# Linear attention times SwiGLU on one core: u's tile, GpSimd additions, ties of the late divisions and the place of x's copies

## The chip, the cores and the metric

The kernel runs on one core of one Trainium2 chip. The metric is the device time of one execution in microseconds (us), a median over several runs. The times of before were 2395.88, 2392.64 and 2393.47 us, median 2393.47. A core has a matrix engine (TensorE, PE in the profile; its weight loads are PEld), a vector engine (VectorE, DVE), a scalar engine (ScalarE, ACT), GpSimd (POOL) and SyncE (SP). Each engine works through its own queue in order. SP and GpSimd also issue the DMAs here.

## The reference

```
xn = layernorm(x)                              # x: 2048 x 1024, float32
q, k, v = split(xn @ wqkv)                     # 32 heads of 32
pq, pk = phi(q), phi(k)                        # phi(t) = where(t > 0, t + 1, exp(t)) + 1e-6
kv = sum over tokens of pk x v;  z = sum over tokens of pk
o = (pq @ kv) / (pq . z + 1e-6)
s = o @ wo
h = silu(xn @ w1) * (xn @ w3)                  # 3584 columns
out = x + s * silu(h @ w2)
```

All large products are float32. The kernel computes each as three matmuls of a reduced float32 format: an operand is split into a high part (a copy that rounds) and a low part (the rest), and high x high, high x low and low x high are added (`mm3`, lines 97 to 99).

## The kernel before, in words

**Seven products in place of eight.** Every large matrix product is cut into 2 x 2 blocks and computed by Strassen's scheme in Winograd's form: seven block products, with sums of blocks formed ahead (S1 to S4 of the left operand, T1 to T4 of the right) and sums of products behind. A left block is 128 x 128 a piece, a right block 128 x 512 a piece.

**First half ("era 1").** Tokens go in two halves of 1024. For each half, `gemm` (line 399) computes keys, values, queries and then, in 14 pairs of columns, gate (names with g) and up (names with u). The hidden rows h = silu(gate) * up are stored to DRAM (`ho_d`) by GpSimd's DMA queue, together with their sums S1 to S4: `use_up` (line 621) multiplies, and when both parts of a half are there, `sums` (line 631) runs `four_sums` (line 601), four VectorE operations on 128 x 256 each, and stores them (line 635). `pq_d` keeps the queries' phi, `r_d` the reciprocal denominators. Side work (sums of w2's blocks, the product of kv with wo, denominators, divisions) is written as `Job`s and handed out one step at a time by `catch_up` (line 387) after each product.

**The divisions.** `divide` (line 753) loads a block of queries and the matching reciprocals (four DMAs, lines 762 and 764), multiplies them (line 770, VectorE), forms the four sums (VectorE) and has GpSimd store the result (`qs_d`, line 773). Those of the second half of the tokens (16 jobs, `late_work`, line 915) are done in the second era, with two buffers, five empty steps between a job's start and its multiplication. `catch_up(*marks)` ties the step's instructions behind the marks: on the mark's engine, each comes later in the queue than the mark. It is no wait across engines.

**Second half ("era 2", from line 851).** Five segments follow each other: B0 to B3 multiply h by w2 (over 6, 6, 8 and 8 blocks of 128 hidden rows, so 3, 3, 4 and 4 pairs of blocks k), and s multiplies the divided queries by kv x wo. Each goes over 8 groups m of 256 tokens, and in a group over the seven products in the order B11, T2, B21, T1, T3, B22, T4 (the names of the right operands). The right operands of a segment stay in SBUF, one tile a name; a segment's successor is loaded and split during the last group (m = 7), each as its predecessor's last product ends (`right`, line 872: SP loads, ScalarE makes the high part, VectorE the low part). The left operands are loaded and split four products ahead (`fetch(j + AHEAD)`, `left`, line 881), in five buffers. The sums over segments stand in `acc[m]` (four blocks c11, c12, c21, c22 of 128 x 512 a group).

`layer_tokens` (line 935) is the group of B0 to B3. After product B11 (PSUM bank ba), ScalarE copies it to u (line 948); after T2 (bb), VectorE adds bb to u (line 950), ScalarE copies u into bank bc (line 951), and VectorE adds u to c12 (line 953, not in B0). The product B21 then goes on in bank ba, so it can only start when u's copy is done. T1 goes to bd, T3 adds to bc, B22 to bd (after bd was added to c22, line 945), T4 to bc; VectorE adds each to its sum (lines 945, 959, 961).

**Memory.** Era 2's pools take the place of era 1's; a tile waits until the earlier tiles at its address are done with. Era 1 has, from the start of the pools, `pb` (8 x 4 KB a partition), `pe` (3 x 2), `pc` (6 x 2 of tag "c", which hold hs among others, and 4 x 2 of tag "sg", which hold sg), `pa` (7 x 16, the left operands), `praw` (2 x 8 "raw", the loaded weights, and 3 x 4 "job"), `st`. Era 2 has `pacc` (acc0 to acc6, 56 KB), `pu` (u, 2), `pw` (7 x 16, right operands), `pacc2` (acc7, 8), `pt` (2 x 4), `px` (5 x 4). So u lies at 56 to 58 KB, on the last "sg" buffer, and acc7 at 170 to 178 KB, on the first "raw" buffer.

**The order of the work.** Instructions are put in order by a scheduler that follows a model of their times and takes what it holds ready, by priority in the order of the program. At the change of eras, `behind(late[j], first)` (lines 1023 to 1037) puts the last steps of era 1 behind the low parts of the first four right operands of B0 on VectorE: c21 behind B11's, c12 behind T2's, the sums of one half behind B21's, those of the other half behind T1's.

**x.** `lay_x(m)` (line 920) copies 256 rows of x (1 MB) from the input to the output in DRAM, tied behind the last load; s is later added to it by accumulating DMAs. This is done for groups 0 to 6, after each group of segment B2. The last group adds x itself.

Of the kernel before, what the change touches and what calls it, by code (L numbers as in the profile page):

```python
# [9 lines left out]
F32 = mybir.dt.float32  # L10
# [12 lines left out]
def tile_linear_attention_times_swiglu(  # L23
# [576 lines left out]

    def four_sums(x1, x2, s12, s34):

        a11, a21 = (x1.rearrange("p (g t s) -> p g t s", t=2, s=P)[:, :, t] for t in range(2))
        a12, a22 = (x2.rearrange("p (g t s) -> p g t s", t=2, s=P)[:, :, t] for t in range(2))
        s1, s2 = (s12.rearrange("p (g n s) -> p g n s", n=2, s=P)[:, :, n] for n in range(2))
        s3, s4 = (s34.rearrange("p (g n s) -> p g n s", n=2, s=P)[:, :, n] for n in range(2))
        yield [nc.vector.tensor_add(out=s1, in0=a21, in1=a22),
               nc.vector.tensor_sub(out=s2, in0=s1, in1=a11)]  # L608
        yield [nc.vector.tensor_sub(out=s3, in0=a11, in1=a21),
               nc.vector.tensor_sub(out=s4, in0=a12, in1=s2)]  # L610

    def hidden(h, pair):
        sg = {}
        i = [f1 > 2 * pair for f0, f1 in FB].index(True)
        k = pair - FB[i][0] // 2

        def use_gate(n, c, src):
            sg[n, c] = signed(f"sg{h}_{pair}_{n}{c}")
            nc.scalar.activation(sg[n, c], src, AF.Silu)

        def use_up(n, c, src):
            nc.vector.tensor_mul(out=sg[n, c], in0=src, in1=sg[n, c])  # L622
            halves = sg[n, c].rearrange("p (g t s) -> p g t s", t=2, s=P)
            if n == 0:
                nc.gpsimd.dma_start(out=ho_d[i][2 * h + c][:, :, 0, k], in_=halves[:, :, 0])  # L625
            else:
                nc.gpsimd.dma_start(out=ho_d[i][2 * h + c][:, :, 1:3, k], in_=halves)  # L627
            if (n, c) in ((0, 1), (1, 0)):
                sums(c)

        def sums(c):
            o = [small(f"hs{h}_{pair}_{c}_{e}") for e in range(2)]
            for e, done in enumerate(four_sums(sg[0, c], sg[1, c], *o)):
                made[f"{h}_{pair}_", c, e] = done
                nc.gpsimd.dma_start(out=ho_d[i][2 * h + c][:, :, 3 + 2 * e:5 + 2 * e, k],  # L635
                                in_=o[e].rearrange("p (g n s) -> p g n s", n=2, s=P))

        return use_gate, use_up
# [218 lines left out]
    def late_pool(name, bufs=1):  # L857
        return ctx.enter_context(tc.tile_pool(name=name, bufs=bufs, reuse_waits="tile"))

    pacc, pu, pw, pacc2, pt, px = (late_pool(*how) for how in (  # L860
        ("pacc",), ("pu",), ("pw",), ("pacc2",), ("pt", 2), ("px", 5)))

    class Segment:
# [17 lines left out]
        def left(self, m, n):  # L881
            t = px.tile([P, 2, ND // 2, P], FR, tag="x", name=f"X{PARTNER[n]}{self.name}_{m}")
            x_ = t[:, :, :self.nk]
            loads[:] = [nc.sync.dma_start(out=x_[:, 1].bitcast(F32), in_=self.left_of(m, PARTNER[n]))]
            made[m, n, self.name] = split(x_[:, e] for e in range(2))
            return x_
# [6 lines left out]
    def split(pair):  # L893
        hi, lo = pair
        src = lo.bitcast(F32)
        nc.scalar.copy(out=hi, in_=src)  # L896
        return nc.vector.tensor_sub(out=lo, in0=src, in1=hi.bitcast(F32))  # L897

# [10 lines left out]
    segments = layers + [attention]  # L909
    acc = [(pacc if m < NG - 1 else pacc2).tile([P, 2, 2, C], F32, tag=f"acc{m}", name=f"acc{m}") for m in range(NG)]  # L910

# [5 lines left out]

    jobs.append((late_work(), False))

    def lay_x(m):  # L920
# [14 lines left out]
    def layer_tokens(seg, m, first):  # L935
        name = f"{seg.name}_{m}"
        V, A = nc.vector, nc.scalar
        c11, c12, c21, c22 = (acc[m][:, t, n] for t in range(2) for n in range(2))
        ba, bb, bc, bd = (bank(f"{n}{name}") for n in "abcd")
# [12 lines left out]
        if not first:  # L952
            V.tensor_add(out=c12, in0=c12, in1=u)
        yield ba, False
# [11 lines left out]
    def attention_tokens(seg, m):  # L966
        name = f"{seg.name}_{m}"
        V, A = nc.vector, nc.scalar
        a11, a12, a21, a22 = (acc[m][:, t, n] for t in range(2) for n in range(2))
        ba, bb, bc, bd = (bank(f"{n}{name}") for n in "abcd")  # L970
# [52 lines left out]
    def behind(late, first):  # L1023
        for i in late:
            tc.add_manual_dep(i.ins, first.ins.name, mybir.DependencyInfo(
                mybir.DependencyClass.NoSync, mybir.DependencyReason.DATA))

    tail = f"{NH - 1}_{NF // 2 - 1}_"
    late = [[made["u" + tail, "c21"]], [made["u" + tail, "c12"]], made[tail, 1, 0] + made[tail, 1, 1],
            made[tail, 0, 0] + made[tail, 0, 1]]  # L1030
    with tc.high_priority(offset=150):
        for j, n in enumerate(ORDER):
            if j < AHEAD:
                fetch(j)
# [43 lines left out]
```

## Time and profile before

| what | value |
|---|---|
| median of 3 runs | 2393.47 us (2392.64 to 2395.88) |
| the profiled execution | 2394.54 us, its span 2392.8 us |
| mean granted clock of TensorE | 0.996 |
| ScalarE busy | 957.0 us, 40% |
| GpSimd busy | 287.9 us, 12% |
| VectorE busy | 1659.7 us, 69% |
| bytes moved by DMAs | 395.45 MB, mean 165 GB/s |

How to read it. Times in the trace are microseconds from the start of the span. A row of the timeline has the start, the duration, the engine, the line of the kernel, the operation, out<-in, the shapes, how many were merged, and in brackets how long the engine had been idle before and what ended that. A row of the stretches ("windows") has the stretch, its length, the busy time and number of instructions of PE, PEld, DVE, ACT and POOL, the granted clock of TensorE (1.00 is full), the DMA engines' share and GB/s. A row of the waits has the engine, what it wanted to do, whom it waited for, the total, the count and the longest. Consecutive operations of one engine overlap a little, so their distance is less than their duration. Names: XS4B is the left operand S4 in a segment B, B21B the right operand B21, aB to dB the four PSUM banks, qd the queries being divided, hs the sums and sg the product silu(gate) * up.

The product of a segment with 3 pairs of blocks is 9 matmuls, with 4 pairs 12.

### The profile page before, as it was taken

What the parts mean: (1) busy time and instruction counts of PE and PEld (TensorE: products, weight loads), DVE (VectorE), ACT (ScalarE), POOL (GpSimd) and SP (SyncE); (2) the same over time, 40 slices, a digit from 0 to 9 for tenths busy, and PEclk for the clock granted to TensorE, in tenths of its full rate; (3) what the DMA queues carried; (4) which work ended last, traced back from release to release, by engine and by line L of the source; (5) the groups of instructions that cost most, each with busy time, mean ns of one, the idle gap of its engine ahead of it and who ended that gap; (6) DMA issues with size and microseconds to landing.
All of it is one profiled execution on the core that took longest, in us unless ns stands there. A gap on an engine that the chain in (4) does not pass through costs nothing.

```text
span 2392.8 us, 29793 instructions
## 1 busy us (share of the span) xinstructions
PE 2337.6 (98%) x10544; PEld 1927.8 (81%) x10544; DVE 1659.7 (69%) x2948; ACT 957.0 (40%) x1619; POOL 287.9 (12%) x357
## 2 busy tenths in 40 slices
PE   6999999999999999999999999999999999999999
PEld 5788888888888888887888888887777778788787
DVE  8755787888887666567777787787446675754744
ACT  5434554433332244355343333344343342444532
POOL 3000111211112100000232221211000000000010
PEclk9999999999999999999999999999999999999999
DMA  3211455567664593124354556435355666833766
GB/s 124 88 53 36 158 188 165 192 224 244 228 224 145 183 336 104 64 106 132 139 176 161 188 173 200 159 113 178 99 157 176 208 238 215 282 114 97 234 150 159
DMA packets 266406, 395.45 MB, mean 165 GB/s; under 512 B 17120, under 2 KB 191456, under 8 KB 266144
## 3 DMA queue, kind: packets, MB, share of 16 engines
q1 hardware_dynamic: 238576, 302.04, 39.2%
q0 software_dynamic: 27680, 91.51, 10.9%
q8 instruction: 82, 1.34, 0.2%
q14 instruction: 68, 0.56, 0.1%
HBM read 271.58 MB, written 140.25 MB: 172 GB/s over the span
## 4 chain that ended last, share of the span: by engine, by line
PE 90%; DMA 4%; DVE 3%; issue 1%; POOL 1%; ACT 1%; SPq 1%; DVEq 0%; ACTq 0%; POOLq 0%
PE dB L97 2%; PE dB L99 2%; PE aB L97 2%; PE dB L98 2%; PE aB L99 2%; PE aB L98 2%; PE cB L97 2%; PE cB L99 2%; PE cB L98 2%; PE kv L514 1%; PE bB L97 1%; PE bB L98 1%; DMA qd<-pq_d 1%; PE bB L99 1%; PE den L740 1%
## 5 line engine op out<-in xcount | busy, mean ns | idle before, releaser
L635 POOL DMA_DIRECT2D ho_d<-hs x112 | 101.9, 911 | 80.2 <-DVE hs L608 56.7
L627 POOL DMA_DIRECT2D ho_d<-sg x56 | 51.1, 912 | 460.4 <-DVE sg L622 430.2
L773 POOL DMA_DIRECT2D qs_d<-qd x32 | 27.4, 859 | 500.3 <-DVE qd L610 322.7
L586 POOL DMA_DIRECT2D pq_d<-pq x32 | 17.6, 552 | 488.5 <-DVE pq L475 485.3
L625 POOL DMA_DIRECT2D ho_d<-sg x56 | 37.9, 676 | 141.8 <-DVE sg L622 129.9
L97 PE MATMUL aB<-B21B,XA12B 128*128 128x512 f32 x112 | 44.5, 397 | 7.4 <-ACT uB L948 7.4
L897 DVE TENSOR_TENSOR XS1B<-XS1B 128x384 fp32r<-128x384 f32 (+1 forms) x32 | 20.0, 623 | 43.9 <-ACT XS1B L896 43.8
L99 PE MATMUL dB<-T1B,XS1B 128*128 128x512 f32 x112 | 43.9, 392 | 3.5 <-DVE XS1B L897 3.5
L97 PE MATMUL aB<-B11B,XA11B 128*128 128x512 f32 x112 | 44.2, 394 | 2.7 <-ACT XA11B L896 2.4
L97 PE MATMUL dB<-B22B,XS4B 128*128 128x512 f32 x112 | 44.3, 396 | 2.5 <-DVE acc L945 1.8
L770 DVE SCALAR_TENSOR_TENSOR qd<-qd 128x512 f32<-128x512 f32 x32 | 22.0, 688 | 35.6 <-DMA qd<-pq_d 34.0
L99 PE MATMUL bB<-T2B,XS2B 128*128 128x512 f32 x112 | 43.9, 392 | 1.6 <-DVE XS2B L897 1.6
L99 PE MATMUL aB<-B11B,XA11B 128*128 128x512 f32 x112 | 43.9, 392 | 1.1 <-DVE XA11B L897 1.1
L99 PE MATMUL cB<-T3B,XS3B 128*128 128x512 f32 x112 | 44.0, 393 | 0.6 <-DVE XS3B L897 0.6
L99 PE MATMUL aB<-B21B,XA12B 128*128 128x512 f32 x112 | 44.6, 398 | 0.0
L97 PE MATMUL cB<-T3B,XS3B 128*128 128x512 f32 x112 | 44.0, 393 | 0.6 <-ACT cB L951 0.5
L99 PE MATMUL cB<-T4B,XA22B 128*128 128x512 f32 x112 | 43.7, 390 | 0.8 <-DVE XA22B L897 0.8
L98 PE MATMUL aB<-B21B,XA12B 128*128 128x512 f32 x112 | 44.3, 396 | 0.0
L97 PE MATMUL bB<-T2B,XS2B 128*128 128x512 f32 x112 | 43.9, 392 | 0.3 <-ACT XS2B L896 0.2
L97 PE MATMUL dB<-T1B,XS1B 128*128 128x512 f32 x112 | 43.9, 392 | 0.3 <-ACT XS1B L896 0.2
L97 PE MATMUL cB<-T4B,XA22B 128*128 128x512 f32 x112 | 43.7, 390 | 0.2 <-DVE acc L959 0.2
L98 PE MATMUL dB<-B22B,XS4B 128*128 128x512 f32 x112 | 43.7, 390 | 0.0
(5746 smaller groups left out, 8064.4 us busy)
## 6 DMA issues: line engine op xcount, KB each, us to landing
ho_d<-hs POOLq DMA_DIRECT2D x112, 256.0 KB, 4.9
qs_d<-qd POOLq DMA_DIRECT2D x32, 512.0 KB, 4.3
ho_d<-sg POOLq DMA_DIRECT2D x56, 256.0 KB, 3.1
w<-in_B_w SPq DMA_DIRECT2D x56, 256.0 KB
wt_d<-w SPq DMA_DIRECT2D x28, 512.0 KB
pq_d<-pq POOLq DMA_DIRECT2D x32, 256.0 KB, 3.2
a_dS<-xo SPq DMA_DIRECT2D x16, 512.0 KB
pqd<-pq_d SPq DMA_DIRECT2D x16, 512.0 KB
```

Of the source, the lines that this page charges most:

```text
L97: nc.tensor.matmul(acc, lhsT=wh, rhs=ah, start=start, stop=False, skip_group_check=True)
L98: nc.tensor.matmul(acc, lhsT=wh, rhs=al, start=False, stop=False, skip_group_check=True)
L99: nc.tensor.matmul(acc, lhsT=wl, rhs=ah, start=False, stop=stop, skip_group_check=True)
L514: nc.tensor.matmul(acc, lhsT=r[:, 1, t], rhs=r[:, 0, t], start=t == 0, stop=t == C // P - 1)
L586: nc.gpsimd.dma_start(out=pq_d[j // JG][2 * h + c][:, j % JG], in_=pq)
L625: nc.gpsimd.dma_start(out=ho_d[i][2 * h + c][:, :, 0, k], in_=halves[:, :, 0])
L627: nc.gpsimd.dma_start(out=ho_d[i][2 * h + c][:, :, 1:3, k], in_=halves)
L635: nc.gpsimd.dma_start(out=ho_d[i][2 * h + c][:, :, 3 + 2 * e:5 + 2 * e, k], in_=o[e].rearrange("p (g n s) -> p g n s", n=2, s=P))
L740: nc.tensor.matmul(den[0], lhsT=zb[0][:, o:o + P], rhs=a[e][:, i], skip_group_check=True, start=j + e + i == 0, stop=j + e == ND - 1 and i ...
L770: nc.vector.scalar_tensor_tensor(t[:, :2], t[:, :2], 1e-6, t[:, 2:], op0=ALU.add, op1=ALU.mult)
L773: nc.gpsimd.dma_start(out=qs_d[m][:, :, k], in_=t.rearrange("p a (n s) -> p (a n) s", s=P))
L897: return nc.vector.tensor_sub(out=lo, in0=src, in1=hi.bitcast(F32))
```

## The change

Five things change, all in the handling of era 2 and of the last step of era 1.

1. u's pool is put behind `pacc2`. acc7 keeps two of its blocks (4 KB) in `pacc2`; its other two are tiles of their own, `end0` in `pacc2` and `end1` in `pacc`, where u was. By the sizes above u comes to lie at 176 to 178 KB.
2. The four sums of the very last pair of hidden columns run on GpSimd in place of VectorE (8 operations in all), and their ties behind the divisions of B21 and T1 go. Two ties stay: c21 behind B11's, c12 behind T2's.
3. The addition of u to c12 (line 953, 24 times) runs on GpSimd.
4. The steps of the late divisions are tied behind the split of the left operand fetched in the same step (ScalarE's high part and VectorE's low part), as well as behind its load.
5. x is laid after groups 2 to 5 of B1 (four copies) and groups 2 to 4 of B2 (three), in place of groups 0 to 6 of B2.

```diff
-    def four_sums(x1, x2, s12, s34):
+    def four_sums(x1, x2, s12, s34, e=nc.vector):
...
-        yield [nc.vector.tensor_add(out=s1, in0=a21, in1=a22),
-               nc.vector.tensor_sub(out=s2, in0=s1, in1=a11)]
-        yield [nc.vector.tensor_sub(out=s3, in0=a11, in1=a21),
-               nc.vector.tensor_sub(out=s4, in0=a12, in1=s2)]
+        e.tensor_add(out=s1, in0=a21, in1=a22)
+        e.tensor_sub(out=s2, in0=s1, in1=a11)
+        yield
+        e.tensor_sub(out=s3, in0=a11, in1=a21)
+        e.tensor_sub(out=s4, in0=a12, in1=s2)
+        yield
...
-            for e, done in enumerate(four_sums(sg[0, c], sg[1, c], *o)):
-                made[f"{h}_{pair}_", c, e] = done
+            last = h == NH - 1 and pair == NF // 2 - 1
+            for e, _ in enumerate(four_sums(sg[0, c], sg[1, c], *o, nc.gpsimd if last else nc.vector)):
...
-    pacc, pu, pw, pacc2, pt, px = (late_pool(*how) for how in (
-        ("pacc",), ("pu",), ("pw",), ("pacc2",), ("pt", 2), ("px", 5)))
+    pacc, pw, pacc2, pu, pt, px = (late_pool(*how) for how in (
+        ("pacc",), ("pw",), ("pacc2",), ("pu",), ("pt", 2), ("px", 5)))
...
-            made[m, n, self.name] = split(x_[:, e] for e in range(2))
+            made[segments.index(self), m, n] = split(x_[:, e] for e in range(2))
...
-        nc.scalar.copy(out=hi, in_=src)
-        return nc.vector.tensor_sub(out=lo, in0=src, in1=hi.bitcast(F32))
+        high = nc.scalar.copy(out=hi, in_=src)
+        return high, nc.vector.tensor_sub(out=lo, in0=src, in1=hi.bitcast(F32))
...
-    acc = [(pacc if m < NG - 1 else pacc2).tile([P, 2, 2, C], F32, tag=f"acc{m}", name=f"acc{m}") for m in range(NG)]
+    acc = [(pacc if m < NG - 1 else pacc2).tile([P, 2 if m < NG - 1 else 1, 2, C], F32, tag=f"acc{m}", name=f"acc{m}")
+           for m in range(NG)]
+    end = [(pacc2, pacc)[n].tile([P, C], F32, tag=f"end{n}", name=f"end{n}") for n in range(2)]
+
+    def sums(m):
+        if m < NG - 1:
+            return (acc[m][:, t, n] for t in range(2) for n in range(2))
+        return acc[m][:, 0, 0], acc[m][:, 0, 1], *end
...
-            V.tensor_add(out=c12, in0=c12, in1=u)
+            nc.gpsimd.tensor_add(out=c12, in0=c12, in1=u)
...
     def behind(late, first):
-        for i in late:
-            tc.add_manual_dep(i.ins, first.ins.name, mybir.DependencyInfo(
-                mybir.DependencyClass.NoSync, mybir.DependencyReason.DATA))
+        tc.add_manual_dep(late.ins, first.ins.name, mybir.DependencyInfo(
+            mybir.DependencyClass.NoSync, mybir.DependencyReason.DATA))
...
-    late = [[made["u" + tail, "c21"]], [made["u" + tail, "c12"]], made[tail, 1, 0] + made[tail, 1, 1],
-            made[tail, 0, 0] + made[tail, 0, 1]]
+    late = [made["u" + tail, "c21"], made["u" + tail, "c12"]]
...
-            first = layers[0].right(n)
-            if j < AHEAD:
-                behind(late[j], first)
+            _, low = layers[0].right(n)
+            if j < len(late):
+                behind(late[j], low)
...
                 elif m and 0 < i < len(layers):
-                    catch_up(*loads)
+                    catch_up(*loads, *made[sequence[j + AHEAD]])
             next(parts)
-            if i == 2 and m < ADDED:
-                lay_x(m)
+            if i in (1, 2) and 1 < m < 6 and len(laid) < ADDED:
+                lay_x(len(laid))
+                laid.append(m)
```

`layer_tokens` and `attention_tokens` take their four blocks from `sums(m)`.

More of the change, by code (lines that the diff above doesn't have):

```diff
@@ L918, in tile_linear_attention_times_swiglu @@
     jobs.append((late_work(), False))
+    laid = []
     def lay_x(m):
@@ L937, in layer_tokens @@
         V, A = nc.vector, nc.scalar
-        c11, c12, c21, c22 = (acc[m][:, t, n] for t in range(2) for n in range(2))
+        c11, c12, c21, c22 = sums(m)
         ba, bb, bc, bd = (bank(f"{n}{name}") for n in "abcd")
@@ L968, in attention_tokens @@
         V, A = nc.vector, nc.scalar
-        a11, a12, a21, a22 = (acc[m][:, t, n] for t in range(2) for n in range(2))
+        a11, a12, a21, a22 = sums(m)
         ba, bb, bc, bd = (bank(f"{n}{name}") for n in "abcd")
```

## The prediction

> **What bounds the kernel now.** I read the page first: busy time by engine, then the waits of TensorE, then TensorE's busy time by stretches, then the timeline where those lose most.
>
> ```profile
> span 2392.8 us, 29793 instructions
> PE 2337.6 (98%) x10544; PEld 1927.8 (81%) x10544; DVE 1659.7 (69%) x2948; ACT 957.0 (40%) x1619; POOL 287.9 (12%) x357
> 1668.00:1790.00 122.00, 113.80 (x490) 92.35 (x489) 58.26 (x98) 52.29 (x100) 4.55 (x5) 0.97 0.42 126
> 1790.00:1808.00 18.00, 15.88 (x62) 10.75 (x61) 16.50 (x25) 12.81 (x22) 0.00 (x0) 1.00 0.68 250
> 1808.00:1905.00 97.00, 93.26 (x406) 75.57 (x406) 61.00 (x128) 29.61 (x58) 6.79 (x8) 1.00 0.57 175
> 1905.00:1935.00 30.00, 24.99 (x102) 18.14 (x101) 27.80 (x34) 21.29 (x28) 0.00 (x0) 1.00 0.91 338
> 1935.00:2062.00 127.00, 126.81 (x558) 104.13 (x558) 70.73 (x129) 34.24 (x58) 5.93 (x7) 1.00 0.66 207
> 2062.00:2092.00 30.00, 27.60 (x116) 20.93 (x114) 27.25 (x33) 22.14 (x29) 0.00 (x0) 1.00 0.92 350
> 2092.00:2220.00 128.00, 128.00 (x566) 105.97 (x566) 64.16 (x101) 53.11 (x89) 0.85 (x1) 1.00 0.40 113
> ```
>
> TensorE is the bound: 55 us of the span are not its own, and no edit here touches its work. So only its stops can be won or added to. In each stretch the first number after the length is TensorE's busy time. The change acts from the hand-over of the first half of the kernel to the second (about 1668) to about 2092. There TensorE stands 8.2 us in the first stretch, 2.1 around the step from segment B0 to B1, 3.7 inside B1, 5.0 at B1 to B2, 0.2 inside B2, 2.4 at B2 to B3, none inside B3. Full pace is 128.00/566 = 0.226 us a matmul: 9 x 0.226 = 2.04 us a product in B0 and B1 (3 blocks of k), 2.71 in B2 and B3.
>
> **The hand-over: u's tile.**
>
> ```profile
> 1670.62 0.39 PE L99 MATMUL bB<-T2B,XS2B 128*128 128x512 f32 x1
> 1677.36 0.42 DVE L608 TENSOR_TENSOR hs<-hs,sg 128x256 f32<-128x256 f32 x1
> 1677.81 0.59 ACT L948 COPY uB<-aB 128x512 f32<-128x512 f32 x1 [3.05 <-DVE hs L608]
> 1678.45 0.80 PE L97 MATMUL aB<-B21B,XA12B 128*128 128x512 f32 x1 [7.44 <-ACT uB L948]
> 1682.45 0.43 PE L97 MATMUL dB<-T1B,XS1B 128*128 128x512 f32 x1
> 1646.60 0.69 DVE L90 TENSOR_TENSOR B22u__13440<-wu__13179,B22u__13440 128x512 fp32r<-128x512 f32 x1
> ```
>
> TensorE could go on at 1670.62 + 0.23 = 1670.85; it goes on at 1678.45, 7.6 later. It waits for u's copy, and that starts as the last L608 ends (1677.78). By the pools' sizes u lies at 56 to 58 KB of a partition, on the last of the four "sg" buffers, and L608 is the last reader of one of those. The nine matmuls that follow take 4.00 us in place of 2.04: 1.96 more. So 9.6 us hang on this wait.
>
> After the change u lies at 176 to 178 KB, in the second half of the first "raw" buffer. The last weights are read from there by 1647.3 (last row), so that wait is gone. What is late next?
>
> ```profile
> 1669.40 1.57 ACT L896 CAST B22B<-B22B 128x1024 fp32r<-128x1024 f32 x2 [1.28 <-DMA B22B<-wt_d]
> 1672.37 1.57 ACT L896 CAST T4B<-T4B 128x1024 fp32r<-128x1024 f32 x2 [1.39 <-DMA T4B<-wt_d]
> L897 DVE TENSOR_TENSOR T4B<-T4B x2: 686/954/1221, 1677.7 to 1678.8; 128x1024 fp32r<-128x1024 f32 x1, 128x512 fp32r<-128x512 f32 x1
> 1668.93 0.42 DVE L607 TENSOR_TENSOR hs<-sg,sg 128x256 f32<-128x256 f32 x1
> ```
>
> First ScalarE: if B22B's cast stays ahead of the copy, the copy runs from 1670.97 to 1671.56 and TensorE loses 0.7. If T4B's cast is ahead of it too, the copy ends at 1674.5 and 3.7 are lost. Then VectorE, which is busy without a pause here. Seven of the eight sums end before T4B's division into high and low parts ends (1679.5); back to back a sum holds it 0.34, so 2.3 us go. u's addition (0.6) and two left splits (0.5 each) come forward into that room: T4B is done at about 1678.8, and its product may start at 1671.56 + 4 x 2.04 = 1679.7. That leaves about 1 us against what the sums cost on GpSimd.
>
> ```profile
> 34.54 1.29 POOL L204 TENSOR_TENSOR xb<-xa,xb 128x512 f32<-128x512 f32 x1
> 51.21 1.60 POOL L204 TENSOR_TENSOR xb<-xa,xb 128x512 f32<-128x512 f32 x1
> 52.20 1.16 DVE L326 TENSOR_TENSOR wk__644<-wk__644 128x512 f32<-128x512 f32 x1
> 55.08 1.30 DVE L90 TENSOR_TENSOR T1k__647<-wk__644,T1k__647 128x512 fp32r<-128x512 f32 x1
> 56.90 0.68 DVE L326 TENSOR_TENSOR wk__644<-wk__644 128x512 f32<-128x512 f32 x1
> L953 DVE TENSOR_TENSOR acc<-acc,uB x24: 683/685/693, 1800.5 to 2222.5; 128x512 f32<-128x512 f32 x24
> ```
>
> A GpSimd addition of 128x512 takes 1.29, beside VectorE's operations 1.60; VectorE's own 0.68 becomes 1.16 and 1.30, 0.5 to 0.6 more. A sum is half that size: 0.25 to 0.3 of VectorE's time each, 2.2 for eight. So moving the sums gives back about what it saves, and T4B comes some 1 us late. Value: 9.6 - 0.7 - 0.9 = 8.0 gained. Ends: 9.6 (no stop), and 3.9 (a stop of 3.7 that again slows nine matmuls, 9.6 - 3.7 - 2.0). GpSimd's queue also issues the stores of the hidden rows between the sums; nothing before segment B3's later groups reads them. The two ties left (c21 behind B11's division, c12 behind T2's) stand as in the trace.
>
> **u's addition to c12.** 24 additions of 0.69 leave VectorE and become GpSimd's, 1.3 to 1.6 each. Its reader, the addition of the B22 product, comes products later; u's next writer comes a group later. GpSimd is nearly empty (5.93 of 127 us); only the issues that store divided queries stand behind it. Inside the segments VectorE has room (70.73 of 127), so neither saving nor lock shows. At three steps between segments it stands just ahead of the split that TensorE waits for:
>
> ```profile
> 2086.06 0.69 DVE L953 TENSOR_TENSOR acc<-acc,uB 128x512 f32<-128x512 f32 x1
> 2088.40 0.68 DVE L897 TENSOR_TENSOR XS1B<-XS1B 128x512 fp32r<-128x512 f32 x1
> 2089.14 0.50 PE L99 MATMUL dB<-T1B,XS1B 128*128 128x512 f32 x1 [1.20 <-DVE XS1B L897]
> ```
>
> There 0.6 is saved and 0.5 to 0.6 is locked: value 0. Ends: 3 x 0.6 = 1.8 gained (no lock met), 3 x (1.29 - 0.69) = 1.8 lost (a whole addition waited for).
>
> [...]
>
> **The late divisions.** Each multiplies loaded queries (L770) and then sums them.
>
> ```profile
> DVE qd L770 <- DMA qd<-pq_d: 26.2, 14, 3.0
> 1836.55 0.69 DVE L770 SCALAR_TENSOR_TENSOR qd<-qd 128x512 f32<-128x512 f32 x1 [2.19 <-DMA qd<-pq_d]
> 1839.58 0.50 PE L97 MATMUL dB<-B22B,XS4B 128*128 128x512 f32 x1 [0.73 <-DVE acc L945]
> 1867.08 0.50 PE L97 MATMUL cB<-T3B,XS3B 128*128 128x512 f32 x1 [0.28 <-ACT cB L951]
> qd<-pq_d SPq DMA_DIRECT2D x64, 128.0 KB
> 1816.57 0.37 SPq L884 DMA_DIRECT2D XS4B<-ho_d  x1
> 1822.24 0.51 ACT L896 CAST XS4B<-XS4B 128x384 fp32r<-128x384 f32 x1 [7.18 <-DMA XS4B<-ho_d]
> 1823.82 0.50 PE L97 MATMUL aB<-B11B,XA11B 128*128 128x512 f32 x1 [2.44 <-ACT XA11B L896]
> ```
>
> VectorE's queue puts L770 ahead of additions and splits that are ready, and stands there for its load: 26.2 us in the window 1810 to 2110. Tied behind the split of the left operand four products ahead, it comes some products later, its load long landed. Counting steps, the first division moves from group 1's end to group 2's fourth product. The loads are tied as before, to SP's loads alone; a later division frees its buffer later, so its successor's load comes later too, with six products between. In B1 TensorE stands 3.74, of which 2.44 is another matter: eight loads of 128 KB issued in one burst ahead of XS4B's, and that stays. The rest, 1.3, plus 0.1 for each of four restarts (0.50 for a matmul in place of 0.39), is what goes: 1.7. Ends: 0 (the divisions' 1.8 us then sit before other needed splits) and 3.0 (the burst's stop shrinks as well).
>
> **x laid elsewhere.** Seven copies of 1 MB leave the ends of B2's groups 0 to 6; four go to B1's groups 2 to 5, three to B2's groups 2 to 4.
>
> ```profile
> 2055.53 0.58 SPq L923 DMA_DIRECT2D out<-in_A_x  x1
> 2069.80 0.50 PE L99 MATMUL cB<-T3B,XS3B 128*128 128x512 f32 x1 [0.61 <-DVE XS3B L897]
> 1984.20 0.32 SPq L884 DMA_DIRECT2D XS4B<-ho_d  x1
> 1990.45 0.62 ACT L896 CAST XS4B<-XS4B 128x512 fp32r<-128x512 f32 x1 [3.39 <-DMA XS4B<-ho_d]
> ```
>
> The last one before stood on SP just ahead of B3's right operands, and XS3B came late behind it: 0.8 gained (0.61 and a restart); up to 2.4, that whole step. In B1 the loads run four products ahead: 8.1 us, against 10.9 in B2. The slowest load I found behind a copy and four query loads took 6.25 to its cast; with cast and split 7.6: it still fits. Value: 0.5 lost. Ends: 0, and 10.4, if each of four copies costs what the burst of the same size cost (2.44 and a restart).
>
> **Sum.** -8.0 - 1.7 - 0.8 + 0.5 + 0 = -10.0. The profiled execution took 2394.54 (span 2392.8): it becomes 2384.5 (span 2382.8). The median of the runs, 2393.47, lies 1.07 below it: 2383.5.
>
> **The rivals.**
> (1) The hand-over keeps half: u's copy is queued behind T4B's cast. For it: casts of later operands stood ahead of the copy before, though then it was not ready. Against: it is ready when the first product ends, 1670.62 + 0.39 - 2.04 = 1669.0, and T4B's cast still waits for its load until 1672.37. -3.9 - 1.7 - 0.8 + 0.5 = -5.9: 2387.6. Chance 0.14. [...]
> (2) The copies in B1 delay left operands: 9.9 more, 2393.4, no change. For it: the burst; against: 0.19 us of stops among six copies in B2. Chance 0.07.
> (3) [...] Chance 0.04.
> (4) u does not come free: some tile at its new place is held as long. Then -1.7 - 0.8 + 0.5: 2391.5. Against: the row at 1646.60. Chance 0.05.
>
> **The numbers.** The forecast has 0.70. Between its bounds it reaches 2379 (no stop at the hand-over, and half of the other gains' upper ends) and about 2387; with rival 1 and a little lost beside it, 2390. That holds 8 in 10. A measurement of this kernel can tell about 0.2%, 4.8 us: faster is below 2388.7. Faster: 0.70 and 0.10 of rival 1. Same: the rest of rival 1, rivals 2 and 4. Slower: rival 3.
>
> **What would show it.** Right: the idle before B21B's first matmul under 2 us, no stretch at a granted clock of 0.50 there, VectorE's waits for query loads under 5 us, no more than 1 us of new stops behind copies in B1, GpSimd's c12 additions at 1.3 to 1.8. Wrong: u's copy again released by something later than the first product; left operands landing later than 8.1 us after their issue in B1; splits of 0.69 stretched to 1.3 just before stops of TensorE.

## The result, and the profile after

| | median us | lowest to highest | runs |
|---|---|---|---|
| before | 2394.68 | 2392.64 to 2398.61 | 4 |
| after | 2414.43 | 2409.47 to 2419.16 | 4 |

The changed kernel is slower: ratio 1.008, with a 95% interval of 1.0054 to 1.0107. The prediction was 2383.5, with a range of 2379 to 2390, and faster.

I compare the profiles in the order in which the prediction read that of before. First the page's span and busy times, then the same seven stretches, with their borders moved to where the same groups stand in the changed kernel. The columns of the stretches are as before: length, busy time (and instructions) of PE, PEld, DVE, ACT and POOL, granted clock, share of the DMA engines, GB/s.

```profile
span 2417.4 us, 29786 instructions
PE 2350.6 (97%) x10544; PEld 1937.1 (80%) x10544; DVE 1658.8 (69%) x2916; ACT 954.2 (39%) x1619; POOL 330.1 (14%) x389
```

```profile
1668.00:1790.00 122.00, 116.27 (x491) 93.20 (x490) 61.30 (x90) 55.97 (x104) 10.06 (x13) 0.97 0.42 127
1790.00:1808.00 18.00, 15.94 (x66) 11.87 (x66) 17.11 (x24) 11.68 (x21) 2.19 (x1) 1.00 0.68 245
1808.00:1914.00 106.00, 96.76 (x400) 76.97 (x399) 55.41 (x111) 28.93 (x57) 13.51 (x12) 0.95 0.58 186
1914.00:1948.00 34.00, 27.53 (x97) 20.25 (x96) 26.90 (x32) 21.45 (x28) 3.48 (x2) 0.86 0.82 305
1948.00:2088.00 140.00, 135.00 (x581) 109.77 (x581) 69.74 (x124) 36.89 (x61) 14.81 (x13) 0.99 0.53 173
2088.00:2118.00 30.00, 26.07 (x105) 20.38 (x105) 28.51 (x34) 20.10 (x27) 3.87 (x2) 0.94 0.78 286
2118.00:2246.00 128.00, 128.00 (x567) 105.98 (x566) 68.85 (x104) 53.41 (x89) 10.35 (x9) 1.00 0.41 122
```

The seven stretches are 578 us long in place of 552: the whole loss lies in them. Two things make it up. TensorE stands 32.4 us in them (578 less 545.57 busy), before 21.7: 10.8 more. And its busy time is 15.2 longer (545.57 against 530.34), with only 7 matmuls more inside the borders (1.6 us at 0.226). The clock column tells what the other 13.6 are. Before, only the first stretch was under 1.00 (0.97). Now five are: 0.05 x 106, 0.14 x 34, 0.01 x 140 and 0.06 x 30 make 13.3 us of lost clock that before did not have. So each microsecond of new stops came with somewhat more than another of slow matmuls, and that part looks like busy TensorE.

Who is late is in the waits, first those of SP's queue, then those of TensorE, both of the window 1790 to 2160, and last, from the trace of before, the one wait of TensorE for XA11B that stood there. A row has the engine, whom it waited for, the total, the count, the longest.

```profile
SPq L764 <- DMA qs_d<-qd: 42.3, 14, 5.7
...
PE aB L97 <- ACT XA11B L898: 9.9, 5, 2.6
PE dB L99 <- DVE XS1B L899: 5.4, 3, 2.2
PE cB L97 <- ACT cB L962: 4.5, 3, 2.8
PE dB L97 <- DVE end L956: 3.7, 2, 2.7
...
PE aB L97 <- ACT XA11B L896: 2.4, 1, 2.4
```

The first row is new. L764 is the first load for the next division (L762 of before); it waits for the store of divided queries (L773, now L775). Before had no such wait in this window. What before had there, VectorE's waits for query loads (27.6 us in this window, 26.2 in the prediction's shorter one), is gone: no multiplication (L772, was L770) waits for its load any more. So the tie did what it was meant to do at its own place, and a longer wait appeared on another queue. Of TensorE's waits, that for the first product's left operand XA11B came once before (2.4 us), and comes five times now (9.9).

### The profile page after: what moved, and what is told of

It is laid out like the page before. It is cut to its first block, busy times and chain, and to the rows that moved or that the text cites. A ratio compares the mean times of both kernels' runs of the same rounds, so it can differ in the third digit from the quotient of the medians.

```text
span 2417.4 us, 29786 instructions
## 1 busy us (share of the span) xinstructions
PE 2350.6 (97%) x10544; PEld 1937.1 (80%) x10544; DVE 1658.8 (69%) x2916; ACT 954.2 (39%) x1619; POOL 330.1 (14%) x389
## 3 DMA queue, kind: packets, MB, share of 16 engines
q0 software_dynamic: 27680, 91.51, 10.8%
## 4 chain that ended last, share of the span: by engine, by line
PE 88%; DMA 4%; DVE 3%; issue 2%; ACT 1%; POOL 1%; SPq 1%; DVEq 0%; ACTq 0%; POOLq 0%
PE dB L99 2%; PE dB L97 2%; PE dB L98 2%; PE aB L97 2%; PE aB L99 2%; PE cB L97 2%; PE aB L98 2%; PE cB L99 2%; PE cB L98 2%; PE kv L514 1%; DMA XS3B<-ho_d 1%; DMA qs_d<-qd 1%; PE bB L97 1%; PE bB L98 1%; PE bB L99 1%
## 5 line engine op out<-in xcount | busy, mean ns | idle before, releaser
L964 POOL TENSOR_TENSOR acc<-acc,uB 128x512 f32<-128x512 f32 x24 | 36.3, 1513 | 381.1 <-DVE uB L961 380.1
L775 POOL DMA_DIRECT2D qs_d<-qd x32 | 27.6, 865 | 216.7 <-DVE qd L611 152.6
L97 PE MATMUL aB<-B11B,XA11B 128*128 128x512 f32 x112 | 45.9, 410 | 9.9 <-ACT XA11B L898 9.9
L99 PE MATMUL dB<-T1B,XS1B 128*128 128x512 f32 x112 | 45.2, 403 | 5.4 <-DVE XS1B L899 5.4
L97 PE MATMUL dB<-B22B,XS4B 128*128 128x512 f32 x112 | 45.5, 406 | 4.7 <-DVE end L956 3.7
L97 PE MATMUL cB<-T3B,XS3B 128*128 128x512 f32 x112 | 45.2, 404 | 4.5 <-ACT cB L962 4.5
L99 PE MATMUL aB<-B11B,XA11B 128*128 128x512 f32 x112 | 45.3, 405 | 3.1 <-DVE XA11B L899 3.1
L98 PE MATMUL dB<-T1B,XS1B 128*128 128x512 f32 x112 | 45.0, 402 | 1.7 <-DVE T1B L899 1.7
L899 DVE TENSOR_TENSOR XA12B<-XA12B 128x384 fp32r<-128x384 f32 (+1 forms) x32 | 19.9, 622 | 37.8 <-ACT XA12B L898 37.7
L99 PE MATMUL dB<-B22B,XS4B 128*128 128x512 f32 x112 | 45.0, 402 | 0.7 <-DVE XS4B L899 0.7
L98 PE MATMUL cB<-T3B,XS3B 128*128 128x512 f32 x112 | 44.9, 401 | 0.7 <-DVE T3B L899 0.7
L98 PE MATMUL aB<-B11B,XA11B 128*128 128x512 f32 x112 | 45.3, 404 | 0.0
L97 PE MATMUL dB<-T1B,XS1B 128*128 128x512 f32 x112 | 45.0, 402 | 0.1
L899 DVE TENSOR_TENSOR XS3B<-XS3B 128x384 fp32r<-128x384 f32 (+1 forms) x32 | 21.1, 659 | 34.8 <-ACT XS3B L898 34.8
L99 PE MATMUL cB<-T3B,XS3B 128*128 128x512 f32 x112 | 45.0, 401 | 0.0
L98 PE MATMUL dB<-B22B,XS4B 128*128 128x512 f32 x112 | 44.9, 401 | 0.0
L99 PE MATMUL bB<-T2B,XS2B 128*128 128x512 f32 x112 | 44.1, 394 | 0.5 <-DVE XS2B L899 0.5
```

The costliest lines, as they stand in the source:

```text
L97: nc.tensor.matmul(acc, lhsT=wh, rhs=ah, start=start, stop=False, skip_group_check=True)
L98: nc.tensor.matmul(acc, lhsT=wh, rhs=al, start=False, stop=False, skip_group_check=True)
L99: nc.tensor.matmul(acc, lhsT=wl, rhs=ah, start=False, stop=stop, skip_group_check=True)
L775: nc.gpsimd.dma_start(out=qs_d[m][:, :, k], in_=t.rearrange("p a (n s) -> p (a n) s", s=P))
L899: return high, nc.vector.tensor_sub(out=lo, in0=src, in1=hi.bitcast(F32))
L964: nc.gpsimd.tensor_add(out=c12, in0=c12, in1=u)
```

## Experiments

Two theories stood against each other after the profile. **The queue:** tied divisions come later, so their stores come later, so the loads for later divisions stand at the head of SP's queue, and the left operands' loads stand behind them. **The held splits:** GpSimd's additions hold VectorE's splits, and the late operands come from there. The place of x's copies was a third possible cause. "Before" in each table is the kernel before, run on the same chip in the same session; the row of after has its own, 2394.68. Lateness means, in the profiles, where u's addition of one group stands, counted from the addition of c21 (1664.25 in the trace of before, 1664.23 in that of after), less the same of before; it leaves out what the first half of the kernel varies by. It comes from one execution of each kernel, and u's addition is VectorE's, so it can also move by what VectorE waits for. Line numbers shift by a few lines from kernel to kernel: the first load of a division (its reciprocals) is L762 in before, L764 in after, L767 in e6 and e10; the loads of left operands are L884, L886, L889.

**1. The change without one part each.** The tie undone (e1_no_tie):

```diff
-                    catch_up(*loads, *made[sequence[j + AHEAD]])
+                    catch_up(*loads)
```

> The changed kernel with one part undone: the late divisions are tied behind the loads alone, as before the change. Theory (the tie): tied divisions end later, so their two buffers come free later, and the loads of the next queries stand at the head of SP's queue until the store of two jobs before has landed (42.3 us of such waits in the changed kernel, none before), with the left operands' loads behind them. It expects SP's waits for those stores to be 0, the 24 us that are lost from group 5 of B1 to group 2 of B3 to go, and a time of 2387 to 2394. Rival 1 (x's copies in B1 delay the loads) and rival 2 (GpSimd's additions hold VectorE) expect the loss to stay: 2408 or more.

x's copies back after groups 0 to 6 of B2 (e2_lays_back):

```diff
-            if i in (1, 2) and 1 < m < 6 and len(laid) < ADDED:
-                lay_x(len(laid))
-                laid.append(m)
+            if i == 2 and m < ADDED:
+                lay_x(m)
```

> The changed kernel with x laid after groups 0 to 6 of B2 again. The theory of the tie expects little: 2408 to 2420, SP's waits for stores still about 40 us. The rival (x's copies in B1) expects 2395 or less.

c12's addition back on VectorE (e3_c12_vector):

```diff
-            nc.gpsimd.tensor_add(out=c12, in0=c12, in1=u)
+            V.tensor_add(out=c12, in0=c12, in1=u)
```

> The changed kernel with u's addition to c12 on VectorE again (24 additions). The theory of the tie expects 2408 to 2418, and SP's waits for stores still about 40 us. The rival (GpSimd's additions hold VectorE where TensorE waits) expects 2400 or less.

The last pair's sums back on VectorE, without the two ties that went (e4_sums_vector):

```diff
-            for e, _ in enumerate(four_sums(sg[0, c], sg[1, c], *o, nc.gpsimd if last else nc.vector)):
+            for e, _ in enumerate(four_sums(sg[0, c], sg[1, c], *o, nc.vector)):
```

> The changed kernel with the last pair's eight sums on VectorE again, without their old ties. About the hand-over alone: GpSimd's sums stretched the divisions of B21, T1 and T3 by 5.6 us (4.57, 2.10 and 3.21 in place of 1.82, 0.69 and 1.82). [...] If the sums did not matter, group 7 of B0 comes within 1 us of where it is.

Before's median beside all four is 2397.44.

| kernel | median us | ratio to before, 95% | SP's waits for stores | lateness at the end of B0 / in group 3 of B3 |
|---|---|---|---|---|
| after | 2414.43 | 1.008 (1.0054 to 1.0107) | 42.3 | -0.2 / 24.4 |
| e1_no_tie | 2401.38 | 1.0018 (1.0006 to 1.0031) | 0 | 0.3 / 7.3 |
| e2_lays_back | 2421.84 | 1.0118 (1.0085 to 1.015) | 44.9 | 1.4 / 29.1 |
| e3_c12_vector | 2415.03 | 1.0072 (1.0044 to 1.0099) | 37.8 | 0.9 / 17.3 |
| e4_sums_vector | 2411.14 | 1.0058 (1.0036 to 1.0079) | 41.1 | -5.5 / 12.9 |

Only the tie's removal moves the time clear of after's interval; it takes most of the loss with it. Not all: 2387 to 2394 was expected, and even without the tie the kernel is 4 us slower than before. In its trace the waits are as before: SP's wait for stores is gone, and VectorE stands for queries again (its waits, 1790 to 2160).

```profile
DVE qd L772 <- DMA qd<-pq_d: 29.8, 16, 2.7
```

The times of e2, e3 and e4 overlap with after's, so none of these three parts is shown to cost anything by its removal here. In the profiles, sums on VectorE are worth 5.3 us at the hand-over (from -0.2 to -5.5), far more than the 1 us at most that was set for sums that do not matter. That c12 on VectorE is 7.1 better by B3 is not shown: after's profiled execution was its slowest (2419.16), e3's its fastest (2407.85), and their ratios are alike.

**2. The tie alone, and its cure.** Before with nothing but the tie, here to the split's low part on VectorE (e5_tie_alone):

```diff
-            made[m, n, self.name] = split(x_[:, e] for e in range(2))
+            made[segments.index(self), m, n] = split(x_[:, e] for e in range(2))
...
-                    catch_up(*loads)
+                    catch_up(*loads, made[sequence[j + AHEAD]])
```

> The kernel before with the tie alone added: the late divisions also behind the split of the left operand four products ahead. The theory of the tie expects most of the loss from this one edit: 12 to 19 us slower than before (ratio 1.005 to 1.008), SP waiting some 40 us for stores of divided queries. If the tie costs only together with GpSimd's additions and x's new places, the ratio lies within 0.002 of 1.

Measured 2416.6 beside 2396.8: ratio 1.0086 (1.0069 to 1.0103), 19.8 us. That is as much as the whole loss of the change, and more than the 12 to 19 that were expected, by the tie alone, with no GpSimd addition and no copy moved. SP's waits, 1790 to 2160:

```profile
SPq L762 <- DMA qs_d<-qd: 36.9, 12, 7.0
```

One chain from its trace shows how. Rows of SP's queue, VectorE, GpSimd, ScalarE and TensorE in the order of time, between groups 4 and 5 of B1:

```profile
1857.35 0.68 DVE L770 SCALAR_TENSOR_TENSOR qd<-qd 128x512 f32<-128x512 f32 x1
1857.56 0.32 SPq L884 DMA_DIRECT2D XA22B<-ho_d  x1
1859.73 0.84 POOL L773 DMA_DIRECT2D qs_d<-qd  x1 [12.28 <-DMA XA22B<-ho_d]
1863.39 0.54 SPq L762 DMA_DIRECT2D qd<-r_d  x1
...
1865.07 0.47 SPq L764 DMA_DIRECT2D qd<-pq_d  x1
1865.65 0.36 SPq L884 DMA_DIRECT2D XA11B<-ho_d  x1
1866.13 0.36 SPq L884 DMA_DIRECT2D XS2B<-ho_d  x1
...
1869.70 0.51 ACT L896 CAST XA11B<-XA11B 128x384 fp32r<-128x384 f32 x1 [7.53 <-DMA XA11B<-ho_d]
1870.26 0.80 PE L97 MATMUL aB<-B11B,XA11B 128*128 128x512 f32 x1 [3.94 <-ACT XA11B L896]
1870.85 0.63 PE L98 MATMUL aB<-B11B,XA11B 128*128 128x512 f32 x1
```

The third division's multiplication runs at 1857.35, its store is issued at 1859.73, and only as that has landed (3.66 later) does the load that overwrites its buffer, for the fifth division, go out, at 1863.39. From 1857.9 SP issued nothing: 5.5 us. Behind that load and three more stood XA11B's, whose turn on a steady beat of 2.04 us would have been about 1859.6; it goes out at 1865.65, then the next three within 1.4 us. Its product stands 3.94 us, and after that stop a matmul takes 0.63 and they follow each other every 0.43 in place of 0.226: 12 of them, 2.4 us more. In before, XA11B's load for the same group follows XA22B's by 2.04 us (1862.75, 1864.79). The same store and the same load stand there like this:

```profile
1840.49 0.85 POOL L773 DMA_DIRECT2D qs_d<-qd  x1 [13.99 <-DVE qd L610]
1857.49 0.54 SPq L762 DMA_DIRECT2D qd<-r_d  x1
```

The load comes 17.0 us after the store, so the buffer has long been free. Counted from the addition of c21, the tie moved the multiplication by 25.7 us (from 172.3 to 198.0), but the load only by 10.9 (193.2 to 204.1), three left operands further on in SP's order. It is so all along: from a store to the load that follows it in its buffer before has 9.2 us or more, e5 3.4 to 5.3 in all cases but one (9.2).

The cure to test that: after, tie and all, but the loads of the query after next are asked for four steps later, when the store should be done (e6_loads_later):

```diff
-            yield from j.steps(data[i])
-            if i + 2 < len(work):
+            for n, _ in enumerate(j.steps(data[i])):
+                if later and n == later and 0 < i < len(work) - 1:
+                    data.append(work[i + 1].load())
+                yield True
+            if not later and i + 2 < len(work):
...
-        yield from go_on([divide(m, k, temp, 5) for m in range(NG // 2, NG) for k in range(ND // 2)])
+        yield from go_on([divide(m, k, temp, 5) for m in range(NG // 2, NG) for k in range(ND // 2)], 4)
```

> The changed kernel, tie and all, with one suspected wait taken away: the queries of the division after the next are loaded four steps later, when the buffer should be free, so that the load does not stand waiting at the head of SP's queue. If the loss runs through SP's queue, its waits for stores fall from 42 us to under 10, what is lost between group 4 of B1 and group 2 of B3 falls from 23 us to under 8, and the time is 2396 to 2404. If the tie costs through VectorE itself (late divisions in front of needed splits), the time stays at 2408 or more.

SP's waits in its trace, 1790 to 2160:

```profile
SPq L767 <- DMA qs_d<-qd: 15.9, 7, 3.9
```

Measured 2405.71 beside 2396.8: 1.0039 (1.0026 to 1.0052). SP's waits fall from 42.3 to 15.9, and with the tie in place about half of the loss goes (1.008 to 1.0039), two thirds of what the tie's removal takes away (1.0018). The marks that were set are narrowly missed (15.9 us for under 10, 2405.71 for 2404 at most). In the profiled execution (2402.29, where five of its ten runs lie over 2407) its lateness in B3 is 7.1, that of e1 without any tie 7.3. So what costs is, for the most part, not the later division but SP standing for its store; whether the rest comes from the waits that are left was not tested.

**3. u's tile alone, and with the copies.** e7_u_tile_alone is before with u at its new place (`pu` behind `pacc2`, `end0`, `end1`); all else, the four old ties too, stays. e8_u_tile_lays is e7 with the copies of x in the middle groups:

```diff
-            if i == 2 and m < ADDED:
-                lay_x(m)
+            if i in (1, 2) and 1 < m < 6 and len(laid) < ADDED:
+                lay_x(len(laid))
+                laid.append(m)
```

> The kernel before with u's tile alone moved (pools, acc7 in parts); sums, additions, ties and x as before. By the hand-over without GpSimd's sums (5.6 us won there) this is 5 to 7 us faster than before: ratio 0.997 to 0.998. If another wait takes the place of u's once the old ties stand, ratio 0.999 to 1.001.

> As the one before, and x laid in the middle groups of B1 and B2. If the copies in B1 delay left operands, 4 us or more slower than the one before; if the free step from B2 to B3 is worth more, 1 to 3 us faster than it.

Beside before's 2396.8, e7 took 2394.69, ratio 0.999 (0.9976 to 1.0003), and e8 2393.13, ratio 0.9991 (0.9979 to 1.0004). Neither can be told from no change, nor one from the other; of e7's two outcomes it is the second, no gain. In e7's trace 3.9 us are won by the end of B0, but 2.9 go again at the burst of query loads in B1. That stop was 2.44 in before; here it is 2.65, and the clock drops:

```profile
1819.41 0.79 PE L97 MATMUL aB<-B11B,XA11B 128*128 128x512 f32 x1 [2.65 <-ACT XA11B L896]
1820.00 0.63 PE L98 MATMUL aB<-B11B,XA11B 128*128 128x512 f32 x1
1820.43 0.63 PE L97 MATMUL dB<-B22B,XS4B 128*128 128x512 f32 x1
```

Fourteen matmuls follow at half pace there, about 2.8 us; before had none after its 2.44.

**4. Without the burst.** If the burst of eight query loads eats the gain, loads one job at a time should keep it. e9_one_load has u's new tile, the sums and c12 on VectorE, x's copies in B2, no tie, and each division's loads four steps into the job before it:

```diff
-        data = [j.load() for j in work[:2]]
+        data = [j.load() for j in work[:1 if later else 2]]
...
-            yield from j.steps(data[i])
-            if i + 2 < len(work):
+            for n, _ in enumerate(j.steps(data[i])):
+                if n + 1 == later and i + 1 < len(work):
+                    data.append(work[i + 1].load())
+                yield True
+            if not later and i + 2 < len(work):
```

> A version from what the runs point to: u's tile moved, the last sums on VectorE without old ties, c12 on VectorE, x in B2's groups 0 to 6, no tie of the divisions; new: the first two divisions' queries are no longer loaded in one burst, each division's are loaded four steps into the one before. The hand-over gives 5.5 us (as with VectorE's sums), the burst's stop of 2.4 to 2.7 us in B1 goes, with the half clock that followed it where it did. 6 to 9 us faster than before: ratio 0.996 to 0.9975. If the stop only moves to the next pair of loads, 3 to 6 us: 0.9975 to 0.999.

e10_one_load_tie is e9 with the tie (`catch_up(*loads, *made[sequence[j + AHEAD]])`):

> The same with the tie of the divisions. If the tie costs only through loads that stand at SP's head for stores, and those loads now come late enough, SP's waits for stores are under 16 us and the time is within 4 us of the one without the tie. If VectorE's standing for queries mattered, it is 1 to 3 us faster than that one. If the tie's cost does not need SP's queue, it is 10 us or more slower.

e12_one_load_lays is e9 with x's copies in the middle groups:

> As the first of these four, with x laid in the middle groups of B1 and B2. If copies in B1 hold up left operands there, 2 to 5 us slower than the first. If the freed step from B2 to B3 is worth more, 1 to 2 us faster.

e11_c12_alone is before with nothing but c12's addition on GpSimd:

> The kernel before with u's addition to c12 on GpSimd and nothing else. By the prediction (0.6 saved, 0.5 to 0.6 held, at three steps between segments) within 2 us of before, ratio 0.9992 to 1.0008. If GpSimd holds VectorE for more than it saves, as the profiles with and without it in the changed kernel suggest (18 and 25 us late at the end), 3 to 7 us slower: 1.0012 to 1.003.

Before's median beside these is 2396.73.

| kernel | median us | ratio to before, 95% | SP's waits for stores | lateness: end of B0 / group 4 of B1 / group 3 of B3 |
|---|---|---|---|---|
| e9_one_load | 2397.53 | 1.0001 (0.9989 to 1.0013) | 0 | -3.9 / -11.4 / 3.1 |
| e10_one_load_tie | 2411.1 | 1.0062 (1.0047 to 1.0076) | 33.1 | -5.2 / -6.6 / 17.8 |
| e12_one_load_lays | 2401.51 | 1.0027 (1.0014 to 1.004) | 0 | -3.9 / -11.6 / 4.4 |
| e11_c12_alone | 2401.87 | 1.0021 (1.0009 to 1.0032) | 0 | 0.1 / 1.2 / 4.7 |

e9 does win the burst: by the mark it is 11.4 us ahead in group 4 of B1. Part of that is the mark, since in before u's addition stands behind a division there; TensorE's own matmuls, the same one in both, are some 8 us ahead. But e9 has given all of it back by B3, so the 6 to 9 us that were expected did not come. The stops that before does not have, or has shorter, stand above all before the product B22 of the segments' last groups. TensorE's waits, 1790 to 2160, and two rows of VectorE ahead of the two stops:

```profile
PE dB L97 <- DVE end L959: 4.9, 2, 3.1
...
1899.61 0.69 DVE L775 SCALAR_TENSOR_TENSOR qd<-qd 128x512 f32<-128x512 f32 x1 [3.39 <-DMA qd<-pq_d]
...
2061.78 0.69 DVE L902 TENSOR_TENSOR XS3B<-XS3B 128x512 fp32r<-128x512 f32 x1 [3.54 <-ACT XS3B L901]
```

Ahead of the first stop VectorE stood 3.39 us for a query load and then worked without a pause up to the addition (1906.64) that TensorE waited for. Ahead of the second it stood 3.54 for XS3B, whose load was late; its queue has that split ahead of B11B's two, where before has it behind them (2069.06). That these waits make up the stops is read from one trace and was not tested. The time is that of before. e10 repeats the tie's cost in another surrounding: 13.6 us between e9's and e10's medians, with the same row in SP's waits. The loads did not come late enough there for the buffer to be free (33.1 us, not under 16), so e10 cannot tell whether the tie would cost without these waits; e6 is the run that bears on it.

```profile
SPq L767 <- DMA qs_d<-qd: 33.1, 11, 5.3
```

e12 against e9 puts x's copies in B1 at 4.0 us, with intervals that do not overlap; e8 against e7 shows no such loss. c12 on GpSimd costs 5.1 us by itself (2.2 to 7.7 by the interval), in the range that the second theory gave. No kernel of the twelve beats before by what can be measured.

## Why the prediction was wrong, step by step

**The bound** was read rightly: TensorE's work is the same 10544 matmuls, and only its stops and its clock changed. But stops were priced at their length and a restart of 0.11. Of the added time, 10.8 us are stops and 13.3 lost clock, so a stop cost more than twice its length. Half clock had been counted only behind stops of 3.7 us and more, at the hand-over; that was the author's estimate, from a trace in which it followed one stop, of 7.44. Two small terms do not come out with a restart of 0.11: XS3B's step is then 0.72, not 0.8, and the four copies 10.2, not 10.4; the forecast moves by under 0.1.

**The late divisions** are the step that failed. The text said: "a later division frees its buffer later, so its successor's load comes later too, with six products between". It gave 1.7 us gained, and the worse end was 0. Measured alone (e5): 19.8 lost. The first division moved by 13.7 us, some seven products, as the text had counted, but those behind it by 25 and more, and the successor's load does not come later by as much: the third division's multiplication moved by 25.7 us, the load that follows it by 10.9, and of the 17 us that had lain between store and load 3.7 were left, the time that the store takes. Then the load stands at the head of SP's queue (36.9 us in all) and holds everything behind it. The prediction named what stands behind the tied instruction on VectorE's queue, and never carried the delay on to the queues of the store and the next load. SP's order had been made with an earlier store in mind; that the scheduler's model believed the buffer free there is argued from that order, the wait itself is shown. The test that the prediction set came out as hoped (waits for query loads under 5 us: there are none), and still the kernel lost.

**The hand-over.** That u's copy would be freed was right, and it ran when the first product ended, at 1669.04 (1669.0 in the text), ahead of T4B's cast: rivals 1 and 4 are out. The 8.0 did not come: 0.2 is left at the end of B0. Of its signs, "no stretch at a granted clock of 0.50 there" failed: there are two, from 1679.01 and 1685.83, 3.4 us each. Rows of the hand-over in the changed kernel, of ScalarE, VectorE and GpSimd, and then TensorE's waits from 1660 to 1800:

```profile
1669.04 0.59 ACT L959 COPY uB<-aB 128x512 f32<-128x512 f32 x1 [7.61 <-PE aB L99]
...
1667.77 4.57 DVE L899 TENSOR_TENSOR B21B<-B21B 128x1024 fp32r<-128x1024 f32 x2
1674.60 2.10 DVE L899 TENSOR_TENSOR T1B<-T1B 128x512 fp32r<-128x512 f32 x1
1676.62 3.21 DVE L899 TENSOR_TENSOR T3B<-T3B 128x1024 fp32r<-128x1024 f32 x2
...
1667.55 0.84 POOL L607 TENSOR_TENSOR hs<-sg,sg 128x256 f32<-128x256 f32 x1
1676.50 0.78 POOL L608 TENSOR_TENSOR hs<-hs,sg 128x256 f32<-128x256 f32 x1
```

```profile
PE aB L99 <- DVE XA11B L899: 2.2, 1, 2.2
PE dB L98 <- DVE T1B L899: 1.7, 2, 1.0
```

The same three operations in e4, where VectorE makes the sums itself:

```profile
1668.61 0.68 DVE L899 TENSOR_TENSOR B21B<-B21B 128x512 fp32r<-128x512 f32 x1
...
1671.38 0.68 DVE L899 TENSOR_TENSOR T1B<-T1B 128x512 fp32r<-128x512 f32 x1
...
1672.92 1.82 DVE L899 TENSOR_TENSOR T3B<-T3B 128x1024 fp32r<-128x1024 f32 x2
```

B21B's 4.57 stands against 1.82 for two such halves undisturbed (T3B's row), T1B's 2.10 against 0.68, T3B's 3.21 against 1.82: 5.6 us, where 2.2 were counted. The half-size GpSimd addition takes 0.75 to 0.84, and 5.6 us over the eight of them are 0.7 each: VectorE is held for nearly all of each. The prediction had scaled a delay of 0.5 to 0.6 from two rows of larger operations. What holds VectorE there, the traces do not show. On top, eight slow matmuls follow the three stops of 0.7 to 1.0, and eight more the stop of 2.2.

Not all of it is GpSimd's. The stop of 2.2 for XA11B stands in e4 as well, where VectorE makes the sums (TensorE's waits, 1660 to 1800):

```profile
PE aB L99 <- DVE XA11B L899: 2.2, 1, 2.2
```

In e7 that wait's longest is 2.5. VectorE comes to this split of the next group only behind T4B's and two more, at 1680.08 in e4; the prediction had followed the chain to T4B and no further. Sums on VectorE give 5.5 us by the end of B0 (e4) or 3.9 (e9 and e12, where half clock follows that stop), the old order with u's tile alone 3.9 (e7).

**c12** was put at 0, with ends of 1.8 either way. Measured alone it is 5.1 lost. The additions' length was right: 1.3 to 1.6 in the text, 1.51 in the mean.

The page's group of the changed kernel (busy time, mean ns of one, idle before it):

```profile
L964 POOL TENSOR_TENSOR acc<-acc,uB 128x512 f32<-128x512 f32 x24 | 36.3, 1513 | 381.1 <-DVE uB L961 380.1
```

In e11 the lateness grows in small steps, 1.2 in the middle of B1, 2.8 at the start of B3, 4.7 in its middle. Its trace shows the last of them, at the step from B2 to B3:

```profile
2091.34 2.21 POOL L953 TENSOR_TENSOR acc<-acc,uB 128x512 f32<-128x512 f32 x1 [20.25 <-DVE uB L950]
2092.90 1.73 DVE L897 TENSOR_TENSOR B22B<-B22B 128x1024 fp32r<-128x1024 f32 x1 [0.51 <-ACT B22B L896]
2095.89 0.75 PE L99 MATMUL dB<-T1B,XS1B 128*128 128x512 f32 x1 [1.71 <-DVE XS1B L897]
```

The 0.6 that leaves VectorE is not won: it stands 0.51 for ScalarE's high part of B22B instead. The split then takes 1.73 beside the addition (1.22 in before), so XS1B comes 0.5 later: TensorE stops 1.71, where before has 1.20, and eight matmuls at half pace follow. The step from B1 to B2 has the same 1.71, without the half clock. The other parts of the 4.7, stops of 0.4 to 0.7 in B1 and a longer one for XS3B, were not followed up.

**x's copies** were put at 0.3 gained. Without the tie the runs give no difference (e8, e7) and 4.0 lost (e12, e9); with it, e2 and the changed kernel cannot be told apart. In e12's trace XA11B's stop at 1864.41 is 3.70, in e9's at 1859.17 only 1.46, and a copy stands ahead of the load. That the sign depends on what else stands in SP's queue is a guess; it is not settled. Rival 2's 9.9 is not borne out.

**The rivals.** Slower had a chance of 0.04 (rival 3). Of what GpSimd's additions cost, the runs show 5.6 us of VectorE held at the hand-over, and 5.1 us of time for c12 alone (e11). The cause of most of the loss was among none of the rivals. The tie's part was the place where a wait was moved, and a rival "the wait moves to SP's queue" belonged there: the profile of before already had what it needed, loads of queries and left operands on the one queue, two buffers, and some 17 us from store to load to set against the move.

## What to carry to other kernels

When an instruction is put later, follow what it frees: here multiplication, store, buffer, next load. If that next load stands in an in-order queue that also feeds the bottleneck and does not move back as far, the delay beyond the slack between store and load is passed on to whatever stands behind it (in e5 the multiplication moved by 25.7 us and the load by 10.9, 3.7 of 17.0 were left between store and load, and SP stood 36.9 in all), so compare that slack with the move, and move the load back together with the instruction. A wait that vanishes from an engine with room to spare (27.6 us on VectorE) is no gain until it's known on which queue it stands now. And stops of the bottleneck should be priced with the clock that they may cost (here 13.3 us beside 10.8 of stops), not by their length alone.

## What the runs showed of the hardware

Half clock (0.50 in the record of the granted clock) came after short stops. In the seven stretches before has it once, after 7.44 us. In the changed kernel it follows stops of 2.19 (ending at 1684.76), 2.63 (1822.65), 2.80 (1853.74), 2.72 (1924.30), 1.70 (1945.11), 2.01 (2053.17) and 2.18 (2112.05), and the three of 0.7 to 1.0 close together at the hand-over; in e7 one of 2.65. Yet no slow matmul follows the stop of 2.44 in before, nor those of 2.24 (1877.73) and 2.12 (2013.94) in the changed kernel. There the slow stretches come in two lengths, 3.4 us (7 to 8 matmuls) and 6.8 (13 to 14 matmuls, with part of the stop), and in the record of the granted clock they all start on one grid of 3.41 us. Three cells of that grid in the changed kernel, the first and second one after the other:

```profile
1941.84:1945.25 3.41, 1.57 (x7) 0.66 (x6) 3.11 (x4) 3.41 (x6) 0.94 (x1) 1.00 0.58 203
1945.25:1948.66 3.41, 3.41 (x9) 2.65 (x10) 3.41 (x5) 1.35 (x3) 0.00 (x0) 0.50 0.00 0
...
1873.56:1876.97 3.41, 1.93 (x9) 1.25 (x7) 0.40 (x1) 0.00 (x0) 0.00 (x0) 1.00 0.76 222
```

In the first TensorE stands 1.84 us (3.41 less 1.57), and the next has half the clock. In the third it stands 1.48, because the stop that ends at 1877.73 is spread over two cells, and no half clock follows. Summed up like this, the cells ahead of the eight slow stretches hold 1.67 to 2.72 us of standing, and of the other cells at full clock none holds more than 1.69. In the traces of before, the changed kernel, e1, e4 to e7 and e9 to e11 the least that half clock followed is 1.65 (e5, the cell from 2046.4), the most that it did not is 1.93 (e4, the cell from 1812.1). So in these traces a stop of some 2 us cost clock or not by where it fell.
